# Attention and feed-forward in one kernel: the order of work drawn up again, with other planner costs and limits

## The chip, the cores and the metric

The kernel runs on one core of a Trainium2 chip. The metric is the device time of one execution in microseconds (us). The time before is the median of three runs. The profile is one execution of the same program.

## The reference

Two parts follow each other. First attention: 8 batches, 8 heads, 576 tokens, 64 values per head. The keys and values have 16 extra "beacon" rows in front, which every token sees; among the 576 tokens a token sees itself and those before it. Then a gated feed-forward step over all 4608 tokens: 512 values in, 1536 hidden, 512 out.

```python
k_all = np.concatenate([beacon_k, k], axis=2)          # 16 + 576 rows
scores = scale * np.matmul(q, k_all.transpose(0, 1, 3, 2))
scores = np.where(causal, -1000000000.0, scores)       # beacon columns stay open
scores = scores - scores.max(-1, keepdims=True)
a = np.exp(scores)
a /= a.sum(-1, keepdims=True) + 1e-09
attn = np.matmul(a, v_all)
x = attn.transpose(0, 2, 1, 3).reshape(4608, 512)
out = (np.maximum(x @ w_gate, 0.0) * (x @ w_val)) @ w_out
```

## The kernel before

**Tiling.** The heads of a batch are taken in four pairs, so that one product carries two heads. The queries of a pair lie in a tile `diag`: 64 queries of one head on partitions 0 to 63, 64 of the other on partitions 64 to 127, zeros elsewhere. The scores of 64 tokens of both heads are then one product of 128 rows. The rows of a batch are cut into the blocks A (with the beacon rows), B, C, D and E, 128 rows each or nearly so, and F, the last 16 tokens, for all four pairs at once.

**One step of attention** (`tile_step`, L616 on, and `group`, L713 on). PE makes scores in a PSUM bank (L663; L655 for E, L658 for F in column tiles of 32). DVE adds the mask and takes the minimum (L678, L675). ACT takes the exponential, with its sum (L689). DVE makes the reciprocal (L701). POOL multiplies by it (L708). The result is turned, in batch 0 by PE (L743) and later by a DMA transpose (L754). PE multiplies by the values (L764 in column tiles of 64, L793 for F), and DVE or ACT copies into `xT` (L440, L438).

**Loads.** In each batch SP's queue brings `k0` to `k3` and `q0` to `q3` (one per pair of heads), `v0` to `v4` (blocks of values), `F` (first rows: the first queries and beacon keys) and `L` (last rows). The order is written by hand in `ORDER0` for batch 0, `ORDER1` for batch 1 and `ORDER` for the others. Each load is cast to bf16 (L486, or L442 for values), by an engine of `CASTS` in batch 0 and by POOL later. Keys and queries are then turned by PE (L497) and copied out of the PSUM bank. A query has two copies, one for each half of the partitions (`evict_q`). The nine pieces of the weights are fetched from POOL's queue (L455), each not before a date: `W_FROM` and then every `W_STEP`.

**Feed-forward.** `hidden` makes, for each of 12 blocks, a product with the gate weights and one with the value weights (L831), ACT's relu (L835) and DVE's multiply (L839). `project` multiplies by the third weight (L851), the result is copied to `osb` and stored. The first three batches are cut at 240 columns of 512 (`CUTS`). So feed-forward's first product needs blocks A and B of all four pairs of batch 0.

**Order.** Nothing of the order is written by hand but the lists above. `Plan.order` is a list scheduler that runs while the kernel is built: each `Task` has engines, a planned cost, the tasks it depends on, and the tiles it holds. The scheduler always takes the task that can start first by the planned times; among equals, the one with the lower `prio`. The instructions are then issued in that order. The chip's engines take their own instructions in order, and wait by semaphores; the planned times are not carried to the chip. The functions `c_dve`, `c_exp`, `c_act`, `c_pool` and `c_pe` are planned costs for n columns.

All of PSUM's eight banks belong to one pool, `banks` (one of them is reserved for fillers in the beginning). `F_MOST`, `SC_MOST`, `V_MOST`, `FIRST_MOST` and `SC_FIRST` limit how many of them feed-forward, scores, products with values, and the first batch may hold at once. Where PE would stand idle early on, the scheduler puts in fillers, products that nobody reads (L910). `LAZY` and `LAZY1` keep a product with values waiting, once it is ready, so that several can follow each other: PE's column tiles change between 128 and 64 there. `RANK`, `AHEAD`, `STEPS`, `WHOLE`, `F_RANK`, `HOLD` and `PACE` are priorities and earliest dates of loads and steps.

```python
key = (at, late, t.prio)
...
late = -1 if part and t.part else 1 if not part and at < (could if SLOT_LAZY else t.ready) + t.lazy else 0
```

Of the kernel before, what the change touches and what calls it, by code (L numbers as in the profile page):

```python
# [20 lines left out]
RANK = (-1.46, -25.77, -19.88, -17.37)  # L21
AHEAD = (-24.27, 8.0, -0.29, 8.0)
W_ISSUE = 0.8
W_MOVE = 3.1
W_FROM = 14.62
W_STEP = 2.67
PACKET = 0.005
W_FIRST = 0.9
W_LEAD = 0.7
W_EACH = 3.3  # L30
W_DELAY = 0.5
W_LATE = 0.6
# [6 lines left out]
SWITCH = 0.1  # L39
LAGS = {"PE": 0.22, "ACT": 0.16, "DVE": 0.14, "POOL": 0.1, "DMA": 0.1}  # L40
LAZY = 22.34
LAZY1 = 32.19
SLOT_LAZY = 0
# [3 lines left out]
F_MOST = 5  # L47
# [3 lines left out]
V_MOST = 5  # L51
OUT = -1300.0
ZERO1 = 25.0
ORDER0 = "q0 q1 F k0 k1 k3 v1 q3 k2 q2 v2 v3 L v0 v4"
ORDER1 = "k0 F q0 k2 L k3 q2 v3 q3 k1 v0 v2 q1 v1 v4"
ORDER = "q0 k1 L k0 F q3 k3 q1 v1 k2 v0 v4 v3 q2 v2"
N_ST = 7
F_RANK = (6.53, 8.48, -1.67, 11.78)
CASTS = ('POOL', 'DVE')
N_OSB = 4  # L60
STEPS = {0: [(['AB'], (-4.55, -4.2, -4.25, -5.72)), (['C'], (-2.2, 4.89, 0.9, 1.36)), (['D', 'E'], (-0.26, 1.73, 10.1, -3.41))],
         1: [(['AB'], (4.7, -5.26, -1.44, -4.08)), (['C'], (8.45, 11.63, 1.33, -5.23)), (['D', 'E'], (3.48, 1.1, 9.61, 4.15))],
         2: [(['AB'], (6.63, 0.38, 0.63, -2.81)), (['C', 'D', 'E'], (6.95, 10.43, 5.74, -0.2))]}
WHOLE = (0.99, 5.23, 4.5, 5.2)
CUTS = {0: (240,), 1: (240,), 2: (240,), 3: ()}
LAST_PARTS = 2
FIRST_MOST = 4
PACE0 = 0.0
HOLD = {0: (0.0, 0.0, 0.0), 1: (0.0, 0.0, 35.39)}
PACE = 31.01  # L70
# [50 lines left out]
class Task:  # L121
    def __init__(self, engines, cost, run, deps, holds, prio, lag, part=False, lazy=0.0, move=0.0):
# [23 lines left out]
class Plan:  # L146
# [7 lines left out]
    def add(self, engines, cost, run, deps=(), holds=(), prio=0.0, lag=None, part=False, lazy=0.0, after=0.0, move=0.0):  # L154
        t = Task(engines if isinstance(engines, tuple) else (engines,), cost, run, deps, holds, prio, lag, part, lazy, move)
        t.ready = after
        for d in t.deps:
            d.users.append(t)
        self.tasks.append(t)
        return t  # L160

    def order(self):
# [13 lines left out]
        part = False  # L176
# [3 lines left out]
        def begin(t, e):  # L180
# [9 lines left out]
            return max(at, free[e]), at  # L190

        while True:
            best = None
            for e in queue:
                for t in queue[e]:
# [3 lines left out]
                    at, could = times  # L199
                    late = 0  # L200
                    if e == "PE":
                        late = -1 if part and t.part else 1 if not part and at < (could if SLOT_LAZY else t.ready) + t.lazy else 0
# [11 lines left out]
            if e == "PE" and FILL_FROM < at < self.filled:  # L214
# [3 lines left out]
                if n > 0 and tile is not None:  # L218
                    done.append(Filler(n, tile, self.fill))
            t.start, t.engine = at, e  # L220
# [22 lines left out]
            else:  # L243
                if isinstance(cost, dict):
                    cost = cost[e]
                if e == "PE":
                    cost = cost * (2.0 if at < WARM else 1.012) + SWITCH * (t.part != part)
# [20 lines left out]
def kernel(  # L268
# [93 lines left out]
    def c_exp(n):  # L362
        return 0.255 + 0.0009 * n
# [4 lines left out]
    def c_pool(n):  # L368
        return 0.245 + 0.00083 * n

    def c_pe(n):
        return 0.003 + n / 2400.0
# [95 lines left out]
    def new_batch(b, prio, work):  # L468
# [45 lines left out]
        def load_pair(kind, p, prio):  # L514
# [20 lines left out]
            def evict_q(hh):  # L535
# [3 lines left out]
                def run(x):  # L539
# [7 lines left out]
            t.rows[kind, p] = [add(("ACT", "DVE"), {"ACT": c_act(512) + (0.0 if kind == "k" else 0.12), "DVE": c_dve(512)},  # L547
                                   evict if kind == "k" else evict_q(i), (tu, zeros), (ps, dst), prio[1]) for i in range(halves)]

        def load_rest(kind, prio):  # L550
# [24 lines left out]
            def evict_q(x, hh):  # L575
# [8 lines left out]
            t.rows["q", kind] = [add(("ACT", "DVE"), {"ACT": 0.06 + c_act(n), "DVE": 0.06 + c_dve(n)}, lambda x, hh=hh: evict_q(x, hh),  # L584
                                     (tu, on_zeros.get(b)), (ps, t.diag), prio[1]) for hh in range(2)]
# [30 lines left out]
    def tile_step(t, p, name, ph, sc, prio, after, blocks):  # L616
# [48 lines left out]
        s = add("PE", pe, scores, deps, (sc[0], sc[1], ph, t.kT, t.diag), prio, None, part=name == "F", after=after)  # L665
# [37 lines left out]
        r = add("DVE", 0.15, inverse, sums, (), prio, 0.18)  # L703
# [240 lines left out]
```

## Time and profile before

| what | value |
|---|---|
| median of three runs | 410.61 us (410.17 to 411.67) |
| the profiled execution's own time | 409.49 us |
| its span, first to last instruction | 407.8 us |
| PE busy | 393.8 us (97%), 3276 products recorded |
| DVE, ACT, POOL busy | 320.7, 289.3, 232.6 us |
| first feed-forward product | 28.68 us from the span's start |
| last product | starts at about 402 us |
| TensorE's clock | 0.998 |

The times of the profile are counted from the span's start. PE counts as busy while products are in its pipeline, so a full PE is not a PE at its peak. Idle time of an engine is put down to what ended it. A line of the chain of waits gives start, duration and what ran; a line of the timeline gives start, duration, engine, line, operation, tiles and count, and, in brackets, the idle time before and what ended it.

### The profile page before, as it was taken

The numbers are of one execution on the slowest core, as the hardware profiler recorded it, in microseconds if no ns is written. First come the engines' busy times: TensorE is split into PE (matmuls) and PEld (weight loads), VectorE is DVE, ScalarE is ACT, GpSimd is POOL, SyncE is SP. The second block draws the span as 40 slices with busy tenths as digits, with TensorE's granted clock in tenths as the row PEclk, the third lists the DMA queues.
The fourth block names the chain that finished last, engine by engine and source line by source line (L and its number), as shares of the span: only waits on it lengthen the run. The fifth ranks groups of instructions, "written<-read, shape, count | busy, mean of one in ns | idle before, by whom it ended". The sixth has DMA issues, their size and how long they took to land.

```text
span 407.8 us, 10376 instructions
## 1 busy us (share of the span) xinstructions
PE 393.8 (97%) x3276; PEld 247.2 (61%) x3311; DVE 320.7 (79%) x1159; ACT 289.3 (71%) x959; POOL 232.6 (57%) x434
## 2 busy tenths in 40 slices
PE   7899999999999999999999999999999999999994
PEld 5567867587767877554558744654554544444483
DVE  6899999989989988899998998887988544244251
ACT  6899989789888968797888799898867432033040
POOL 5799786958686758576875956885727200000000
PEclk9999999999999999999999999999999999999999
DMA  7999999999899999899989999999195720200112
GB/s 230 161 206 223 212 210 197 196 233 216 172 205 231 189 196 225 193 239 210 211 193 214 235 186 193 247 201 214 41 162 125 173 67 0 75 29 0 53 54 51
DMA packets 172616, 68.03 MB, mean 167 GB/s; under 512 B 146832, under 2 KB 168080, under 8 KB 172560
## 3 DMA queue, kind: packets, MB, share of 16 engines
q1 hardware_dynamic: 167808, 62.64, 75.9%
q0 software_dynamic: 4752, 4.72, 7.2%
q8 instruction: 26, 0.43, 0.4%
q14 instruction: 30, 0.25, 0.2%
HBM read 38.27 MB, written 9.44 MB: 117 GB/s over the span
## 4 chain that ended last, share of the span: by engine, by line
PE 83%; POOL 5%; DVE 4%; DMA 4%; ACT 2%; issue 2%; SPq 0%; POOLq 0%; DVEq 0%; ACTq 0%
PE f L831 42%; PE f L851 21%; PE f L663 6%; PE f L764 6%; PE f L497 3%; DMA st<-in_v_dram 3%; POOL xT L708 2%; PE f L655 2%; DVE diag L440 1%; PE f L793 1%; POOL h L486 1%; DMA st<-in_q_dram 1%; DVE f L678 1%; PE f L658 1%; POOL pb L708 1%
## 5 line engine op out<-in xcount | busy, mean ns | idle before, releaser
L708 POOL TENSOR_SCALAR pb<-pb,small 128x576 bf16<-128x576 bf16 (+8 forms) x224 | 121.6, 557 | 59.1 <-DVE small L701 50.3
L689 ACT ACTIVATE pb<-f,small 128x64 bf16<-128x64 f32 (+6 forms) x256 | 131.1, 524 | 20.1 <-DVE small L678 16.1
L678 DVE CUSTOM_DVE_ANT_0 f<-f,mask 128x128 f32<-128x128 f32 (+7 forms) x256 | 112.0, 477 | 7.9 <-PE f L663 5.7
L835 ACT ACTIVATE g<-f 128x512 f32<-128x512 f32 (+3 forms) x156 | 71.8, 470 | 65.0 <-PE f L831 64.0
L831 PE MATMUL f<-xT,wv_r 128*128 128x512 bf16 (+3 forms) x616 | 111.8, 313 | 0.5
L831 PE MATMUL f<-xT,wg_r 128*128 128x512 bf16 (+3 forms) x619 | 109.5, 313 | 0.3
L839 DVE TENSOR_TENSOR hT<-g,f 128x512 bf16<-128x512 f32 (+3 forms) x156 | 80.2, 520 | 36.4 <-PE f L831 33.6
L851 PE MATMUL f<-wo_r,hT 128*128 128x512 bf16 (+1 forms) x423 | 102.0, 373 | 1.0
L831 PEld LDWEIGHTS <-wg_r 128*128 128x128 bf16 x624 | 60.0, 98 | 32.5 <-issue 0.2
L831 PEld LDWEIGHTS <-wv_r 128*128 128x128 bf16 x624 | 59.4, 98 | 32.9 <-issue 0.7
L851 PEld LDWEIGHTS <-hT 128*128 128x128 bf16 x444 | 41.5, 98 | 39.1
L689 ACT ACTIVATION_READ_ACCUMULATOR pb<-f,small 128x1 f32 x256 | 53.9, 210 | 0.0
L663 PE MATMUL f<-kT,diag 128*128 128x384 bf16 (+7 forms) x255 | 47.1, 286 | 3.0 <-DVE diag L440 1.6
L678 DVE DVE_READ_ACCUMULATOR2_ANT small<- 128x1 f32 x296 | 41.5, 140 | 0.2 <-issue 0.2
L486 POOL TENSOR_SCALAR h<-st 128x512 bf16<-128x512 f32 x62 | 37.7, 615 | 3.5 <-DMA st<-in_q_dram 1.3
L440 DVE COPY osb<-f 128x512 f32<-128x512 f32 (+1 forms) x26 | 17.6, 677 | 23.0 <-PE f L851 22.7
L708 POOL TENSOR_SCALAR xT<-xT,small 128x64 bf16<-128x64 bf16 (+4 forms) x64 | 27.0, 436 | 9.6 <-ACT xT L689 4.1
L663 PEld LDWEIGHTS <-diag 128*128 128x128 bf16 x256 | 20.4, 98 | 16.3 <-DVE diag L440 2.3
L438 ACT CAST diag<-f 64x512 bf16<-64x512 f32 (+2 forms) x52 | 23.0, 442 | 9.8 <-DVE diag L440 4.2
L497 PE MATMUL f<-ident,h 128*128 128x128 bf16 (+2 forms) x320 | 28.1, 217 | 1.2 <-POOL h L486 0.6
L440 DVE CAST diag<-f 64x512 bf16<-64x512 f32 (+2 forms) x44 | 26.3, 597 | 3.5 <-ACT diag L438 2.0
L689 ACT ACTIVATE xT<-f,small 128x64 bf16<-128x64 f32 (+5 forms) x64 | 27.8, 452 | 1.0 <-DVE small L678 1.0
(67 smaller groups left out, 377.2 us busy)
## 6 DMA issues: line engine op xcount, KB each, us to landing
st<-in_q_dram SPq DMA_DIRECT2D x32, 256.0 KB, 4.3
st<-in_k_dram SPq DMA_DIRECT2D x32, 256.0 KB, 4.5
out_dram<-osb SPq DMA_DIRECT2D x32, 256.0 KB, 2.5
st<-in_v_dram SPq DMA_DIRECT2D x24, 256.0 KB, 4.8
st<-in_v_dram SPq DMA_DIRECT2D x8, 224.0 KB, 4.9
wg_r<-in_moe_w_gate_dram POOLq DMA_DIRECT2D x3, 512.0 KB, 8.2
wv_r<-in_moe_w_val_dram POOLq DMA_DIRECT2D x3, 512.0 KB, 10.2
wo_r<-in_moe_w_out_dram POOLq DMA_DIRECT2D x3, 512.0 KB, 13.6
```

The lines of the kernel that those rows point to most:

```text
L440: nc.vector.tensor_copy(dst, src)
L486: (nc.gpsimd if x.engine == "POOL" else nc.vector).tensor_scalar(to, of, by, 1.0, ALU.mult, ALU.mult)
L497: nc.tensor.matmul(to, h16.tile[:rows, a * P:(a + 1) * P], ident[:rows, :rows], start=True, stop=True)
L663: nc.tensor.matmul(view(i), t.diag.tile[:, p, j * P:j * P + P], kT[:, p, :n], start=True, stop=True)
L678: nc.vector.tensor_tensor_reduce(out=view(i), in0=view(i), in1=msk, scale=1.0, scalar=small["t"][:, 0:1] if name in "EF" else 3.0e38, op0= ...
L689: nc.scalar.activation(ph.tile.rearrange("p a n -> p (a n)")[:, a:a + n], view(i), AF.Exp, bias=small["t"][:, low:low + 1], scale=-1.0, ac ...
L708: (nc.gpsimd if x.engine == "POOL" else nc.vector).tensor_scalar(one, one, small["t"][:, 8 + i:9 + i], 1.0, ALU.mult, ALU.mult)
L764: nc.tensor.matmul(ps.tile[64 * hh:64 * hh + 64, d0:d0 + w], t.v.tile[:rows, c, D * h:D * h + D], rhs(64 * hh), start=(c == 0), stop=(c == ...
L831: nc.tensor.matmul(to, w_r[:, ki, nf * P:(nf + 1) * P], x, start=(ki == 0), stop=(ki == KM - 1))
L835: r = add("ACT", c_act(w), lambda _, psg=psg, g=g: nc.scalar.activation(g.tile[:, :w], psg.tile[:, :w], AF.Relu), (a,), (psg, g), -1000 + ...
L839: hid.append(add("DVE", c_dve(w), lambda _, psv=psv, g=g, nf=nf: nc.vector.tensor_mul(hT[nf].tile[:, c0:c0 + w], g.tile[:, :w], psv.tile[: ...
L851: nc.tensor.matmul(ps.tile[:, :w], hT[nf].tile[:, t0:t0 + P], wo_r[:, nf, n0:n0 + w], start=(nf == 0), stop=(nf == NF - 1))
```

## The change

The planner's costs, lists, dates and limits get other numbers, and some of its rules change. The instructions of the kernel stay, but for their order, the choice among allowed engines, and the fillers.

- The two copies of a query out of one bank, and the three copies of a first or last row, get a dependency on each other in the plan.
- The planned costs of the exponential, POOL's multiply, PE's products, the reciprocal and the copies of turned blocks change, and PE's factor of 1.012 becomes `PE_RATE` of 0.998.
- `ORDER0` begins with `k1`; the other orders, the priorities, dates and paces get other values.
- Feed-forward may hold four banks (five before), products with values seven (five), the first batch's turns six (four). ACT may cast in batch 0.
- A product with values and an F score no longer belong to one kind: an F product with values has no waiting time and no kind of its own, F's scores are kind 3, and products with values kind 1. After a filler the kind is reset.

```diff
-RANK = (-1.46, -25.77, -19.88, -17.37)
-AHEAD = (-24.27, 8.0, -0.29, 8.0)
-W_ISSUE = 0.8
-W_MOVE = 3.1
-W_FROM = 14.62
-W_STEP = 2.67
-PACKET = 0.005
+RANK = (-7.1, -27.26, -24.83, -20.12)
+AHEAD = (-15.22, 1.47, 8.0, 7.48)
+W_ISSUE = 0.834
+W_MOVE = 3.3
+W_FROM = 15.63
+W_STEP = 2.53
+PACKET = 0.004
...
+PE_RATE = 0.998
-LAZY = 22.34
-LAZY1 = 32.19
-SLOT_LAZY = 0
+LAZY = 29.32
+LAZY1 = 11.61
...
-F_MOST = 5
+F_MOST = 4
-V_MOST = 5
+V_MOST = 7
-ORDER0 = "q0 q1 F k0 k1 k3 v1 q3 k2 q2 v2 v3 L v0 v4"
-ORDER1 = "k0 F q0 k2 L k3 q2 v3 q3 k1 v0 v2 q1 v1 v4"
-ORDER = "q0 k1 L k0 F q3 k3 q1 v1 k2 v0 v4 v3 q2 v2"
+ORDER0 = "k1 q0 q1 F k0 v2 v0 v1 q3 q2 k2 k3 v4 L v3"
+ORDER1 = "k0 q3 k2 q2 k3 F k1 q0 v4 v2 q1 v3 L v1 v0"
+ORDER = "k1 L F k0 q0 q3 k3 q1 k2 v0 v4 q2 v1 v3 v2"
-F_RANK = (6.53, 8.48, -1.67, 11.78)
-CASTS = ('POOL', 'DVE')
+F_RANK = (0.33, 8.02, 9.62, 8.82)
+CASTS = ('POOL', 'DVE', 'ACT')
-STEPS = {0: [(['AB'], (-4.55, -4.2, -4.25, -5.72)), (['C'], (-2.2, 4.89, 0.9, 1.36)), (['D', 'E'], (-0.26, 1.73, 10.1, -3.41))],
+STEPS = {0: [(['AB'], (-6.0, -1.43, -5.75, -2.97)), (['C'], (2.99, -2.13, 9.09, 9.58)), (['D', 'E'], (8.05, -5.08, 8.37, -1.22))],
...
-FIRST_MOST = 4
+FIRST_MOST = 6
-HOLD = {0: (0.0, 0.0, 0.0), 1: (0.0, 0.0, 35.39)}
-PACE = 31.01
+HOLD = {0: (0.0, 18.37, 0.0), 1: (41.75, 0.0, 0.0)}
+PACE = 32.26
...
-                    if e == "PE":
-                        late = -1 if part and t.part else 1 if not part and at < (could if SLOT_LAZY else t.ready) + t.lazy else 0
+                    if e == "PE" and t.part:
+                        late = -2 if part == t.part else -1 if part else 1 if at < t.ready + t.lazy else 0
...
-                    cost = cost * (2.0 if at < WARM else 1.012) + SWITCH * (t.part != part)
+                    cost = cost * (2.0 if at < WARM else PE_RATE) + SWITCH * (t.part != part)
...
     def c_exp(n):
-        return 0.255 + 0.0009 * n
+        return 0.23 + 0.00087 * n
     def c_pool(n):
-        return 0.245 + 0.00083 * n
+        return 0.24 + 0.00083 * n
     def c_pe(n):
-        return 0.003 + n / 2400.0
+        return 0.002 + n / 2400.0
...
-            t.rows[kind, p] = [add(("ACT", "DVE"), {...},
-                                   evict if kind == "k" else evict_q(i), (tu, zeros), (ps, dst), prio[1]) for i in range(halves)]
+            t.rows[kind, p] = []
+            for i in range(halves):
+                t.rows[kind, p].append(add(("ACT", "DVE"), {...},
+                                           evict if kind == "k" else evict_q(i), (tu, zeros, *t.rows[kind, p]), (ps, dst), prio[1]))
...
-        s = add("PE", pe, scores, deps, (sc[0], sc[1], ph, t.kT, t.diag), prio, None, part=name == "F", after=after)
+        s = add("PE", pe, scores, deps, (sc[0], sc[1], ph, t.kT, t.diag), prio, None, part=3 if name == "F" else 0, after=after)
...
-        r = add("DVE", 0.15, inverse, sums, (), prio, 0.18)
+        r = add("DVE", 0.08, inverse, sums, (), prio, 0.25)
...
-                     part=True, lazy=LAZY if t.b > 1 else LAZY1 * t.b)
+                     part=0 if what == "F" else 1, lazy=0.0 if what == "F" else LAZY if t.b > 1 else LAZY1 * t.b)
```

## The prediction

> **What bounds the kernel now.** I read the page first: the busy slices and the chain that ended last, by engine.
>
> ```profile
> PE   7899999999999999999999999999999999999994
> DVE  6899999989989988899998998887988544244251
> ACT  6899989789888968797888799898867432033040
> POOL 5799786958686758576875956885727200000000
> ...
> PE 83%; POOL 5%; DVE 4%; DMA 4%; ACT 2%; issue 2%; SPq 0%; POOLq 0%; DVEq 0%; ACTq 0%
> ```
>
> TensorE (PE) is the bound, and from slice 32 on it is alone: the attention engines fall off near 322 us. The table of windows says when PE fills up, and its line L910 (fillers) and the shapes say how much of a full PE is work.
>
> ```profile
> 10.00:20.00 10.00, 8.12 (x82) 6.12 (x81) 8.90 (x43) 7.98 (x33) 7.63 (x16) 1.00 1.02 163
> 20.00:30.00 10.00, 9.51 (x105) 6.48 (x105) 9.80 (x42) 10.00 (x38) 9.82 (x19) 1.00 1.15 204
> 30.00:40.00 10.00, 9.77 (x129) 7.45 (x123) 9.03 (x33) 9.36 (x29) 9.82 (x16) 1.00 1.20 224
> 50.00:60.00 10.00, 9.94 (x84) 7.39 (x82) 9.91 (x39) 8.55 (x35) 7.99 (x18) 1.00 1.23 219
> ```
>
> Columns (window, PE busy, PEld, DVE, ACT, POOL, clock, DMA, GB/s). In the chain, "323.67 8.20 PE f L831 x38" gives 0.216 us for a product of 512 columns, 0.42 ns per column. All columns without fillers (counted by the code, since some records are missing) cost 366 us at that pitch. So of the span of 407.8 some 42 us are not products. By 50 us only 25 us of products are done: 25 of the 42 are lost there. After the last product (402.3 us) come copy and store, 5.5 us, which the diff leaves alone. Between 50 and 403 us there remain some 11 us. So I need two sums: the start, and the small losses after it. The chain through the start, in order of time:
>
> ```profile
> 12.48 0.46 ACT diag L438
> 12.96 0.70 DVE diag L440
> ...
> 14.95 0.55 DVE diag L440
> 15.52 0.58 ACT diag L438
> 16.12 0.97 ACT xT L689 x4
> ...
> 17.70 0.68 POOL h L486
> 18.39 0.74 POOL xT L708 x2
> 19.13 0.59 POOL v L442
> 19.72 0.74 POOL wv_r L455
> ```
>
> Two query copies that read one bank after another, then exponentials, then GpSimd (POOL), which works without a gap from 17.4 to 46.9 us. The first feed-forward product starts at 28.68 us. The waits view names the pairs (total, times, longest):
>
> ```profile
> ACT diag L438 <- DVE diag L440: 4.2, 7, 1.5
> DVE diag L440 <- ACT diag L438: 2.0, 4, 0.8
> ```
>
> **The change part by part.** Nearly all of it alters the planner, so instructions and bytes stay and the order moves. "−" is a gain.
>
> *Copies of one bank follow each other.* The chip does that already: ACT 12.35–12.94, DVE from 12.96; DVE until 15.49, ACT idle 1.46 us until 15.52. The old plan thought both halves ran at once and parked an engine there. The new plan can put other work before the second half. On the chain the parked times are 0.40 and 1.46, so −1.9 at most; at worst the second half comes one exponential later (+0.7). I take −0.9, half of the bound, since all four pairs want ACT at that time. The halves lie in partitions 0–63 and 64–127. The Trainium skill (PSUM — Partial Sum Buffer, "PSUM bank collisions raise a hardware error") says that two engines may use different quadrants of a bank at once; by that the wait would be the program's own, the old plan's picture could be had, and this dependency would gain 0 (sum −1.9). The rows show the second copy waiting, and I go by them.
>
> *ACT may cast in batch 0.* POOL's chain holds two casts of batch 0, 0.68 and 0.59. Gone from there: −1.3. But ACT is busy 10.00 of 10 from 20 us, so a cast on it there costs its 0.55. Ends −1.3 to +0.55; I take −0.4.
>
> *Weights.* The first date goes from 14.62 to 15.63, the last (eight steps) from 35.98 to 35.87. First issues land at 21.75 and 25.26 us and are used at 28.68 and 30.25: 5 us of cover, cost 0; without it +1.0. Each issue holds POOL 0.79; the fifth, issued 27.52 (2.2 after its date of 25.30), moves to about 28, where it may fall behind the last norm the first products need: −0.8 to 0, I take −0.1.
>
> *Load order.* The first five loads are the same set (q0 q1 F k0 k1); only k1 leads, so the first pair still needs four of them: 0. Behind them three values now stand before pairs 2 and 3. In landings of before, the last load that the four pairs need came at 11.85 us (eleven landings at 0.75 to 1.3 us each); it will be the twelfth, near 13.9: +2.05 if that decides. The fourth pair's scores ran only at 18.59 us, some 4 us after load, cast, transpose and copy could be through. Hidden: 0. SP issues all fifteen by 13.7 us either way.
>
> *Dates.* Block C of batch 0 is held to 18.37. Before, the minimums of the first C ran at 11.97 and 13.89 us, 0.45 and 0.49 of DVE between those of A and B: −0.9 if they leave. But D and E of pair 1 now rank −5.08, ahead of A and B of pairs 1 and 3 (−1.43, −2.97), and may take the place: I take −0.2. A and B of batch 1, held to 41.75, were scored at about 45: 0.
>
> *Waits of PE after 50 us.* Only two are real: 0.58 idle at 60.58 (a POOL cast) and 0.56 at 185.36 (a query copy); with their surroundings 1.46. I take −0.7; a new order can as well make two of its own (+1.5).
>
> *Grouping P@V, F apart.* After 50 us PE changes 39 times between column tiles of 128, 64 and 32, each about 0.108 beyond its columns: 4.2. Longer patience for batches 2 to 7 (29.3 against 22.3) may save four bursts of two changes (−0.9); shorter for batch 1 (11.6 against 32.2) may add three (+0.65). I take −0.2.
>
> *Planned durations.* No instruction gets shorter. Rows against old and new figures: exponential of 64, 256, 512 columns starts the next after 0.29, 0.45, 0.66 (old 0.31, 0.49, 0.72; new 0.29, 0.45, 0.68); reciprocal 0.073–0.084 (0.15; 0.08); 512-column product 0.216 (0.219; 0.215). By 28 us some 45 exponentials were planned 0.035 too long: 1.6 us by which later steps were placed wrongly. I take −0.5, ends −1.6 to 0. PE's 1.3% over 350 us is 4.7 us in the plan, but on the chip shows only as the two waits above.
>
> *Feed-forward 4 banks, values 7, first steps 6.* With four, an eviction must end within three groups of the next products: 2.6 us at 512 columns, 1.24 at 240 (0.412 each). DVE's multiply takes 0.61 and 0.32. DVE waited for products here 33.6 us in all, so it is mostly early. I take +0.2; ends 0 and the rival's price below.
>
> *Sum:* −0.9 −0.4 −0.1 −0.2 −0.7 −0.2 −0.5 +0.2 = −2.8 us. A gain in the start carries fully, because PE is full from 50 us on and 80 us of feed-forward alone follow 322; the later weights keep their cover (the ninth block's products ran at 47.99, landed 38.38). The profiled execution took 409.49 us; 406.7 for its like. The median lies 1.1 higher, 410.61: **407.8 us**.
>
> **The rivals.**
>
> *Not carried (no change, 410 us).* POOL's chain from 17.4 to 46.9 us keeps its norms (0.29 to 0.73 each) and nine issues, and batch 1's loads land up to 42.8 us in a full DMA. If these pace the start, only mid-stream −0.7 is left: 409.9. For it: POOL 9.82 of 10. Against: its chain is fed late, by the two query pairs. That the program's waits already put the copies in order, so that the new dependency does nothing, leads here too.
>
> *Four banks hold PE (slower).* In the 240-, 256- and 272-column stages (144 groups), slack is 1.24 − 0.32 − 0.2 = 0.7 us: one DVE minimum of 0.60 (512 columns) ahead of the multiply fits, two do not. That is where it decides. If two stand ahead once in six groups, 24 stops of about 0.25 us make +6; with the other gains left, −3.0+6 = +3.0: 413.6. For it: DVE 9.9 of 10 at 50–60 us. Against: DVE idles 33.6 us for products. The Trainium skill (Perfetto Trace Analysis, "Matmul Optimizations") wants all eight PSUM banks used; this cap speaks against that, though the three to four others go to attention. No row here shows a cap of four.
>
> *Late pairs (slower).* Pairs 2 and 3 come 2.05 us later, their minimums and exponentials pile up behind 16 us where ACT is full, and the weights' 1.0 loses its cover: 410.6+3.0−0.7 = 412.9. Decides if the fourth pair's scores move beyond 20 us.
>
> **How the numbers follow.** Forecast 0.49, not carried 0.27, four banks 0.14, late pairs 0.10. Within 0.5% (about what a measurement tells apart here; 2.05 us) is 408.6 to 412.7. The forecast's own range is 405 to 409.3: the full bounds of start and switches (−1.9 −1.3 −0.9 −1.5) reach −5.6. About a tenth of it ends above 408.6, and as much of "not carried" below; so faster 0.47, same 0.29, slower 0.24. Of the slower cases the cheaper half belongs in the range: 404.8 to 413.6.
>
> **What would show it.** Right: the idle time of ACT and DVE for each other's diag copies falls from 6.2 us to under 3; the first L831 product starts before 28 us; products done by 50 us rise from 25 to 27; PE idle between 50 and 322 us stays under 3; the last product ends at about 400. Wrong: the first product at 28.5 or later; fewer products by 50 us; PE waiting in the 240-column stages for hT or g; more than 45 changes of column tile.

## The result, and the profile after

The changed kernel takes 413.18 us (median of five runs, 412.42 to 414.29), against 410.61 before: a ratio of 1.0058, interval 1.0035 to 1.0082. Forecast were 407.8. The profiled execution took 413.18 us with a span of 411.4, that of before 409.49 and 407.8.

The page of after, the busy slices and the chain by engine:

```profile
PE   7899999999999999999999989999999999999994
DVE  6899989898989889889789898997895844233251
ACT  5898999786979899797669787874884853033040
POOL 5799769657695688568748874982761620000000
...
PE 60%; DVE 3%; issue 2%; POOL 1%; ACT 1%; DMA 1%; SPq 0%; POOLq 0%; ACTq 0%; DVEq 0%
```

The chain of after can be followed back only to 125.18 us, so its shares add up to some 70% and are not to be set against the 83% of before. TensorE (PE) is still the bound (busy 396.4 of 411.4 us), and the last recorded product starts at 405.60 us instead of 401.98. The table of windows (window, PE busy, PEld, DVE, ACT, POOL, clock, DMA, GB/s):

```profile
10.00:20.00 10.00, 8.87 (x91) 6.99 (x91) 8.61 (x39) 8.13 (x28) 7.20 (x12) 1.00 0.84 168
20.00:30.00 10.00, 9.44 (x103) 6.56 (x100) 9.73 (x44) 10.00 (x39) 9.51 (x21) 1.00 1.18 223
30.00:40.00 10.00, 9.16 (x118) 7.04 (x116) 9.61 (x35) 8.40 (x30) 9.73 (x15) 1.00 1.20 231
50.00:60.00 10.00, 9.95 (x86) 7.39 (x85) 9.28 (x48) 9.05 (x38) 5.78 (x13) 1.00 0.69 153
```

PE is busier from 10 to 20 us (8.87 against 8.12), but less than half of what it holds there is work: 3.2 us of it are products that count, against 2.7; the fillers would take 4.1 us at single pitch in after and 4.2 in before. The measure that tells more is the one of the prediction, how far PE lies behind: the time gone, less the columns of all products but fillers that had started by then, at 0.42 ns each (products in column tiles of 64 or 32 run side by side and count by their share of the 128 columns). What it grows by is lost to waits, fillers, changes of column tile, or a slow clock. Some products are missing in the records (35 of 3221 before, 37 in after); each is counted where its weights were loaded. One product of 512 columns is 0.22 us, so differences below that mean nothing. In the profiles:

| at, us | before | after | a_t3 | a_t3l |
|---|---|---|---|---|
| 30 | 20.74 | 21.60 | 21.82 | 20.48 |
| 50 | 24.34 | 25.37 | 26.13 | 24.30 |
| 100 | 27.30 | 27.80 | 28.57 | 26.49 |
| 180 | 30.53 | 32.47 | 32.53 | 30.53 |
| 220 | 32.18 | 33.32 | 33.48 | 31.59 |
| 280 | 34.33 | 38.36 | 36.63 | 34.55 |
| 400 | 36.15 | 39.60 | 38.20 | 36.15 |

(a_t3 and a_t3l are experiments below.) By 400 us after is 3.45 us further behind. Two stretches make up more than that: the start, +1.03 us by 50, and 220 to 280 us, 5.04 instead of 2.15. The others nearly cancel: after wins 0.5 from 50 to 100 and 0.6 from 280 to 400 us, and loses 0.6 from 100 to 220 (1.4 up to 180, of which 0.8 come back). The experiments take the two stretches up after the suspects that the prediction had named. Times in microseconds are medians, and a ratio is to runs of before taken alongside, whose median moved between 410.22 and 410.97 from set to set; compare kernels by their ratios.

### The profile page after: what moved, and what is told of

Read it like the earlier page. It is cut to its first block, busy times and chain, and to the rows that moved or that the text cites. A ratio compares the mean times of both kernels' runs of the same rounds, so it can differ in the third digit from the quotient of the medians.

```text
span 411.4 us, 10350 instructions
## 1 busy us (share of the span) xinstructions
PE 396.4 (96%) x3278; PEld 249.2 (61%) x3315; DVE 320.4 (78%) x1163; ACT 287.0 (70%) x956; POOL 233.7 (57%) x433
## 4 chain that ended last, share of the span: by engine, by line
PE 60%; DVE 3%; issue 2%; POOL 1%; ACT 1%; DMA 1%; SPq 0%; POOLq 0%; ACTq 0%; DVEq 0%
PE f L838 32%; PE f L858 17%; PE f L670 4%; PE f L771 4%; PE f L498 2%; PE f L662 1%; DMA st<-in_beacon_v_dram 1%; ACT pb L696 1%; POOL pb L715 1%; DVE f L685 1%; PE f L800 1%; DVE diag L441 1%; DVE osb L441 0%; DVE small L703 0%; POOL h L487 0%
## 5 line engine op out<-in xcount | busy, mean ns | idle before, releaser
L685 DVE CUSTOM_DVE_ANT_0 f<-f,mask 128x448 f32<-128x448 f32 (+7 forms) x256 | 111.7, 474 | 6.5 <-PE f L670 5.0
L838 PE MATMUL f<-xT,wv_r 128*128 128x512 bf16 (+3 forms) x617 | 110.6, 313 | 0.8 <-ACT pb L696 0.4
L858 PE MATMUL f<-wo_r,hT 128*128 128x512 bf16 (+1 forms) x426 | 100.7, 373 | 0.9
L696 ACT ACTIVATION_READ_ACCUMULATOR pb<-f,small 128x1 f32 x256 | 55.0, 215 | 0.0
L670 PE MATMUL f<-kT,diag 128*128 128x128 bf16 (+4 forms) x255 | 46.0, 286 | 0.8 <-DVE hT L846 0.7
L441 DVE CAST diag<-f 64x512 bf16<-64x512 f32 (+2 forms) x52 | 28.5, 553 | 5.0 <-PE f L498 2.7
L498 PE MATMUL f<-ident,h 128*128 128x128 bf16 (+2 forms) x320 | 29.3, 220 | 3.2 <-POOL h L487 1.5
L498 PEld LDWEIGHTS <-h 128*128 128x128 bf16 (+2 forms) x320 | 21.5, 99 | 15.1 <-POOL h L487 4.4
L682 DVE TENSOR_REDUCE small<-f 128x1 f32<-128x512 f32 x40 | 27.3, 682 | 3.0 <-PE f L662 2.2
L696 ACT ACTIVATE xT<-f,small 128x64 bf16<-128x64 f32 (+3 forms) x64 | 27.6, 446 | 2.4 <-DVE small L685 1.7
```

Source lines behind the costliest of these rows:

```text
L441: nc.vector.tensor_copy(dst, src)
L498: nc.tensor.matmul(to, h16.tile[:rows, a * P:(a + 1) * P], ident[:rows, :rows], start=True, stop=True)
L670: nc.tensor.matmul(view(i), t.diag.tile[:, p, j * P:j * P + P], kT[:, p, :n], start=True, stop=True)
L682: nc.vector.tensor_reduce(out=to, in_=view(i), axis=AX.X, op=ALU.min)
L685: nc.vector.tensor_tensor_reduce(out=view(i), in0=view(i), in1=msk, scale=1.0, scalar=small["t"][:, 0:1] if name in "EF" else 3.0e38, op0= ...
L696: nc.scalar.activation(ph.tile.rearrange("p a n -> p (a n)")[:, a:a + n], view(i), AF.Exp, bias=small["t"][:, low:low + 1], scale=-1.0, ac ...
```

## Experiments: what it was not

**The cap of four banks.** `a_f5` is after with one line changed, `b_f4` is before with the other.

```diff
-F_MOST = 4
+F_MOST = 5
```

> The kernel after, with F_MOST back at 5 (feed-forward may hold five banks again); all else as after, 413.2 us. Theory 'four banks': the cap makes PE wait for banks, so with five the time falls to 410.5 or less and the waits of PE between 50 and 322 us fall under 3 us. Theory 'no slack' (the measured costs let PE's products stand right behind the casts and copies they need, and each small delay on the chip stops PE): the cap is not the cause, the time stays within 412 to 414 and PE's waits name POOL casts (h) and query copies (diag) as in the kernel after. Theory 'start' (the new loads of batch 0 cost 1.2 us by 50 us, the rest is chance): the start is as in after, 413 by 1 either way.

> The kernel before (410.6 us) with F_MOST 4 alone. 'Four banks': slower, 412.5 to 414, with multiplies (hT) and relus (g) ending PE's waits in the 240- and 272-column stages. 'No slack' and 'start': no change, 410 to 411.5, since a group's bank is back within 1.2 us and three groups of 240 columns last 1.24.

Measured: a_f5 413.14, ratio to before 1.0074 (1.0055 to 1.0094); b_f4 410.22, 1.0003 (0.999 to 1.0016). No price of the cap shows in either order. But a_f5 is another order, and loses in another place: 4.0 us from 150 to 180 us, where after loses 1.6 (PE waits 1.02 us at 178.28 for a copy into `xT`), and only 2.2 from 220 to 280, where after loses 5.0.

**The dependency between copies.** `a_nodeps` is after with the copies of one bank independent of each other in the plan again.

```diff
-            t.rows[kind, p] = []
-            for i in range(halves):
-                t.rows[kind, p].append(add(("ACT", "DVE"), {...},
-                                           evict if kind == "k" else evict_q(i), (tu, zeros, *t.rows[kind, p]), (ps, dst), prio[1]))
+            t.rows[kind, p] = [add(("ACT", "DVE"), {...},
+                                   evict if kind == "k" else evict_q(i), (tu, zeros), (ps, dst), prio[1]) for i in range(halves)]
```

> The kernel after without the dependency between the copies of one bank; the planner again takes them for parallel. If the dependency gains what I put on it (0.9 in the start and idle time of ACT and DVE for each other's diag copies), the time rises from 413.2 to 414 or more and those waits rise from some 2 us to 5 or more. If the chip's order of the copies is what counts and not the plan's picture of it, 413 by 0.7 either way. 'No slack': a plan that thinks the copies parallel is tighter still, so 414 to 415.

Measured: 418.26, 1.0189 (1.0164 to 1.0214). The waits view (engine line, what it waited for: total, times, longest) of after, and then of a_nodeps:

```profile
DVE diag L441 <- ACT diag L439: 0.5, 1, 0.5
```

```profile
ACT diag L439 <- DVE diag L441: 7.0, 9, 1.6
...
DVE diag L441 <- ACT diag L439: 2.2, 6, 0.8
```

Before it was 6.2 us, after it is 0.5, and 9.2 without the dependency. So that part of the change does to these waits what was forecast. With the lists of after the kernel is some 5 us slower without it, though the edit also draws the whole order anew, so the waits alone are not shown to cost that. It isn't what made the kernel slower.

**The planned durations.** `b_newcost` is before with all the new planned costs and its own lists, `b_rate` is before with PE's factor alone.

```diff
-                    cost = cost * (2.0 if at < WARM else 1.012) + SWITCH * (t.part != part)
+                    cost = cost * (2.0 if at < WARM else 0.998) + SWITCH * (t.part != part)
```

> The kernel before with the new planned costs alone (exponential, POOL multiply, reciprocal, turned copies, PE's product and factor), lists and limits as before. 'No slack': slower than 410.6 by 2 to 4 us, 412.5 to 414.5, and PE's waits between 50 and 322 us rise from 2.8 idle to 4 or more. If better costs give a better order, as I forecast: 408 to 410. 'Lists fitted to their costs' (priorities and dates were chosen for the old costs, and any redrawn order is worse by chance): also slower, but then the loss lies in the start and in other places than waits for casts.

> The kernel before with PE's factor 0.998 in place of 1.012 alone; priorities and dates as before. The plan gets 1.4% shorter on PE and nothing on the chip does. 'No slack': waits of PE after 50 us rise by 1 to 3 us over the kernel before, time 411.5 to 413.5. 'Lists fitted to their costs': a redrawn order, anywhere from 411 to 418, with most of the loss wherever the order happens to be worse, start included. If a truer PE cost gives a better order: under 410.

Measured: b_newcost 422.05, 1.0292 (1.0269 to 1.0315); b_rate 413.48, 1.0067 (1.0052 to 1.0081). b_rate keeps the start of before (24.63 us behind at 50) and loses later, above all between 220 and 280 us: 33.05 to 38.41 behind, 5.4 us where before loses 2.15. With the old lists, PE's new factor alone makes the kernel slower by as much as the whole change does, and all new costs together by five times as much. Lists and costs go together here: lists drawn up for one set of costs lost under another, twice.

## Experiments: 220 to 280 us

The timeline of after (start, duration, engine, line, operation, tiles, count; in brackets the idle time before and what ended it), PE and then POOL:

```profile
238.10 1.33 PE L498 MATMUL f<-ident,h 128*128 128x128 bf16 x12
239.26 1.03 PE L838 MATMUL f<-xT,wg_r 128*128 128x512 bf16 x4
...
241.07 0.38 PE L498 MATMUL f<-ident,h 128*128 128x128 bf16 x4
241.68 0.38 PE L498 MATMUL f<-ident,h 128*128 128x128 bf16 x4 [0.22 <-ACT diag L439]
242.51 1.02 PE L838 MATMUL f<-xT,wv_r 128*128 128x512 bf16 x4 [0.45 <-ACT pb L696]
```

```profile
237.00 2.96 POOL L487 TENSOR_SCALAR h<-st 128x512 bf16<-128x512 f32 x5
```

Five casts of a batch follow each other on POOL, 0.6 us each, and their turns (L498) follow each other on PE. Twelve turned blocks of 128 columns take 1.33 us there; a group of four takes 0.38. Each turn holds a PSUM bank until its copies are through. At 242.51 a feed-forward product waits 0.45 us, and what ends the wait is an exponential that has read its bank. Before has the turns apart, each between products of the third weight:

```profile
232.72 0.39 PE L497 MATMUL f<-ident,h 128*128 128x128 bf16 x4
232.94 1.03 PE L851 MATMUL f<-wo_r,hT 128*128 128x512 bf16 x4
233.81 0.61 PE L497 MATMUL f<-ident,h 128*128 128x128 bf16 x8
```

`e_turns` moves every turn of batches 1 to 7 back in PE's queue, until it stands at least 0.6 us (planned) behind its cast:

```diff
+    for t in [t for t in made if t.engine == "PE" and t.start > 50.0 and "turned" in t.run.__qualname__]:
+        ...                       # behind the last PE task with u.start < t.ready + 0.6
+        made.insert(to, made.pop(i))
```

> The kernel after with one thing moved: after 50 us, turns of keys and queries (L498) go later in PE's queue where they stood less than 0.6 us behind their cast in the plan; every other engine keeps its order. 'No slack': PE's waits for casts (130, 115, 240, 275 us in the kernel after, some 2.4 us with what is hidden in weight loads) go, the products done between 50 and 400 us gain 1.5 to 2.5 us, and the time falls from 413.2 to 411 to 411.7. If those waits only move (the copies come later and hold ACT, DVE and the scores behind them): 413 by 0.7. 'Start': the loss of 1.2 us by 50 us stays in either case.

Measured: 415.07, 1.0112 (1.0094 to 1.013). No wait of PE for a POOL cast over 0.2 us is left after 50 us, and others came: 0.76 us at 123.93 for a query copy, 0.44 at 245.98 that ends, as at 242.51 above, with an exponential. Here the wait was moved and not cured.

`a_lazy` puts `LAZY` back to 22.34, which redraws the order from 220 us on. `a_t3` gives the turns of later batches a limit of three banks:

```diff
+    t_ps = Share(banks, 3)
...
-            ps = Hold(first_ps if b == 0 else v_ps, 1 + users)
+            ps = Hold(first_ps if b == 0 else t_ps, 1 + users)
```

> The kernel after with LAZY put back from 29.32 to 22.34: the order of instructions is the same until about 220 us, and differs behind it. Theory (PSUM banks): between 236 and 243 us of the profile after, a burst of feed-forward turns and five POOL casts in a row holds PSUM banks, the feed-forward products find none, and TensorE falls behind by about 1.5 to 2 us between 220 and 260 us. With the old LAZY the turns are spread, so this loss goes and the time is 411.3 to 411.8. Rival (the attention's engines set the middle, whatever the turns do): the time stays at 413.2 within 0.5, and the 2 us are lost at another place behind 260 us. Rival (only a start carries): as the second.

> The kernel after with the turns of batches 1 to 3 held to at most three PSUM banks at a time by a limit of their own; the order is that of after until about 233 us. Theory (PSUM banks): a part of the loss between 236 and 243 us goes, 412.3 to 413.0, and the products behind 240 us start at least 0.5 us earlier against the same amount of work. Rival (the order behind 233 us is redrawn and any redraw is as good): within 0.5 of 413.2 on either side, with no gain between 236 and 243 us.

Measured: a_lazy 412.17, 1.0044 (1.0025 to 1.0062); a_t3 411.30, 1.0034 (1.0015 to 1.0054), more than expected. (The interval of a_t3 overlaps that of after, but ten of its twelve runs lie below all five of after.) a_t3's order is that of after until 233 us. PE in a_t3:

```profile
237.43 1.03 PE L859 MATMUL f<-wo_r,hT 128*128 128x512 bf16 x4
238.29 0.39 PE L499 MATMUL f<-ident,h 128*128 128x128 bf16 x4
238.78 1.02 PE L839 MATMUL f<-xT,wg_r 128*128 128x512 bf16 x4
...
242.61 1.89 PE L839 MATMUL f<-xT,wg_r 128*128 128x512 bf16 x8 [0.37 <-ACT pb L697]
```

The burst of twelve has become four and eight, with feed-forward in between. Between 220 and 280 us a_t3 falls 3.15 us further behind, after 5.04. Only a part of these 1.9 us is won at the burst: from 233 to 245 us after falls 2.4 us behind, a_t3 1.8 (before nothing). From 268 to 280 us it is 1.9 against 0.8. There after has a wait for a query copy inside its products with values, and twelve turned blocks that again take longer than in a_t3 (after, then a_t3):

```profile
273.62 1.60 PE L771 MATMUL f<-pTb,v 128*64 128x128 bf16 x32 [0.28 <-DVE diag L441]
275.15 1.16 PE L498 MATMUL f<-ident,h 128*128 128x128 bf16 x12
```

```profile
274.01 0.84 PE L499 MATMUL f<-ident,h 128*128 128x128 bf16 x12
```

So the limit is worth some 1.9 us in this stretch, but that held banks are the cause is not shown: it also draws the order behind 233 us anew, the wait at 242.61 stays, and a_lazy, another order without the limit, loses 3.4 us there, nearly as little as a_t3. What the profile of after shows is the place: where turns follow each other at the pace of their casts PE falls behind, and 0.67 us of idle time there (0.22 and 0.45) end with a copy and an exponential.

## Experiments: the start

`e_cast` moves one POOL cast of batch 0, that of the last key (16.53 us in after), two norms earlier. `a_lazyc` and `a_t3c` add the same to a_lazy and a_t3.

> The kernel after with one POOL instruction moved: the cast of the last pair's load in batch 0 (16.53 us) goes two norms earlier in POOL's queue. 'Late pairs' (the loads of pairs 2 and 3 stand behind three values, land up to 2.6 us later, and their casts fall behind norms in POOL's queue): the first feed-forward product comes 0.3 to 0.9 us earlier than 30.7 and the time falls by as much, to 412.3 to 412.9. If the start is paced by the sum of POOL's work and not by that pair: 413.2 by 0.4, first product at 30.7 still.

> The edit of a_lazy together with that of e_cast (the last pair's POOL cast in batch 0 stands two norms earlier in POOL's queue). If both causes are right and add up (1.2 us of the start, 1.5 to 2 us at 236 to 243 us): 410 to 411, within 0.1% of the kernel before. If a gain in the start does not carry: as a_lazy. If neither matters: 413.2.

> The edit of a_t3 (turns of later batches in at most three PSUM banks) together with that of e_cast (the last pair's POOL cast in batch 0 two norms earlier). Theory (two causes that add up: 1.2 us in the start, 1.9 us of held banks): against a_t3's 411.3 another 0.7 to 1.2 us less, 410.1 to 410.6, no different from the kernel before. Rival (what is won before 50 us is lost again between 100 and 200 us, as in e_cast and a_lazyc): 411.3 to 412.3, with products done by 50 us about 1 us further than in a_t3 and by 180 us no further.

Measured: e_cast 414.58, 1.0099 (1.008 to 1.0118); a_lazyc 412.82, 1.0071 (1.0045 to 1.0097); a_t3c 412.57, 1.0052 (1.0033 to 1.0072). None is faster than its like without the move. e_cast's profile looked like a success at first, 24.56 us behind at 50 instead of 25.37. That reading fell. a_t3l below has no edit ahead of 112 us and shows 24.30 there, while a_t3, with the same start, shows 26.13: the new start differs by up to 2 us from execution to execution. Ten profiles with the new order of loads and fillers show 24.30 to 26.46, 25.5 on average; before, b_f4 and b_rate show 24.24 to 24.63. So the new start costs about 1.1 us on average. And e_cast, whose order on PE is that of after, is level with after again by 180 us (32.47 both).

**What waits at 131 us.** Part of what an execution wins in the start it can lose here. PE, POOL and SP in a_t3c:

```profile
130.73 0.57 PE L839 MATMUL f<-xT,wv_r 128*128 128x240 bf16 x4
132.54 0.40 PE L499 MATMUL f<-ident,h 128*128 128x128 bf16 x4 [1.24 <-POOL h L488]
```

```profile
131.87 0.62 POOL L488 TENSOR_SCALAR h<-st 128x512 bf16<-128x512 f32 x1 [1.33 <-DMA st<-in_k_dram]
```

```profile
126.21 0.42 SPq L522 DMA_DIRECT2D st<-in_k_dram  x1
```

PE waits 1.24 us for a cast, the cast for a key, and the key was issued by SP at 126.21 behind transposes and two stores that had waited for other engines. Nothing held the load itself, as a_t3l shows below by issuing it at 117.93. In after the same wait is 0.44 us. `a_t3l` and `a_t3cl` move this load and the two beside it, in SP's queue alone, ahead of two transposes of xT, one of pTf and two stores:

```diff
 pTb<-pb   (transpose)
+st<-in_q, st<-in_k, st<-in_v
 xT<-xT x2, pTf<-pf   (transposes)
 out<-osb  (store)
-st<-in_q
 out<-osb  (store)
-st<-in_k, st<-in_v
```

> The kernel a_t3 with three loads (a query, a key, a block of values) moved ahead in SP's queue, from about 125 to 127 us to about 119 us, ahead of two transposes of xT, one of pTf and two stores; all other engines keep their order. Theory (the key load behind SP's transposes paces TensorE at 131 us in most executions): the load lands before 126 us, no wait of TensorE for a POOL cast between 125 and 135 us, and 0.3 to 0.8 us less than a_t3: 410.5 to 411.0. Rival (what is gained ahead of 130 us is lost at the next wait anyway; or the transposes, 2 us later now, delay the products with values): 411.3 or slower, up to 412.5.

> The same move of three loads in a_t3c (a_t3 with the last pair's POOL cast in batch 0 two norms earlier; 412.57, with a wait of 1.24 us at 132.5 us). Theory: this queue is what eats the start's gain: 410.0 to 410.8, and products done by 180 us at least 1.2 us further than in a_t3c. Rival (the cast's move itself costs elsewhere, whatever the queue): 411.8 to 412.6, with the wait of 1.24 us gone and the time lost at another place.

Measured: a_t3l 411.01, 1.0003 (0.9982 to 1.0023); a_t3cl 411.64, 1.0017 (0.9992 to 1.0042). In a_t3l:

```profile
117.93 0.42 SPq L522 DMA_DIRECT2D st<-in_k_dram  x1
...
119.42 3.11 SPq L762 DMA_TRANSPOSE xT<-xT  x2
```

The key lands at 121.9 us instead of 131.7 and 130.4 (a_t3c, after), and no wait of PE for a POOL cast is left between 120 and 140 us in either. Both kernels gain 0.3% against their like; the intervals of each pair overlap, so this gain is likely rather than shown. With it, a_t3l is level with the kernel before.

**Why the start varies.** Ahead of the third turn of batch 0 (a query's, whose load is third in the new order) the old order has seven fillers, the new one has one. Before, and then a_t3:

```profile
5.79 1.50 PE L910 MATMUL f<-mask,ident 128*128 128x256 bf16 x7
7.22 0.29 PE L497 MATMUL f<-ident,h 64*128 64x64 bf16 x4
```

```profile
5.44 0.27 PE L918 MATMUL f<-mask,ident 128*128 128x256 bf16 x1
7.78 0.40 PE L499 MATMUL f<-ident,h 128*128 128x128 bf16 x4 [2.07 <-POOL h L488]
...
9.54 1.04 PE L918 MATMUL f<-mask,ident 128*128 128x256 bf16 x4
10.36 0.63 PE L499 MATMUL f<-ident,h 128*128 128x128 bf16 x4
10.79 0.85 PE L918 MATMUL f<-mask,ident 128*128 128x256 bf16 x3
11.43 0.95 PE L671 MATMUL f<-kT,diag 128*128 128x448 bf16 x5
```

Soon after 2.07 us of idle time, fillers and turns at 9.5 to 11.4 us run at twice their pitch (0.213 us for 256 columns), and the granted clock of these windows says so:

```profile
8.00:9.00 1.00, 1.00 (x11) 0.69 (x7) 0.78 (x2) 0.00 (x0) 0.95 (x2) 0.72 1.18 185
9.50:11.40 1.90, 1.90 (x13) 1.47 (x12) 0.81 (x3) 0.58 (x2) 0.64 (x2) 0.50 1.18 227
```

Fourteen fillers stand between that turn and the first scores. In five of ten profiles with the new start they ran slowly and the first score product came at 10.90 to 11.80 us, in the other five at 9.09 to 9.62. In all ten the first products ran at twice their pitch. In the fast five that ended at 4.6 to 5.5 us, and the idle time ahead of the third turn was 0.81 to 1.56 us. In three of the slow (a_lazyc, a_t3, a_t3cl) it ended by 5.4 us too, but the idle time was 1.86 to 2.07 us, and the doubled pitch came back at 8.3 to 9.0 us. In two, after and e_turns, it lasted through to 10.5 and 13.7 us, with idle times of 0.52 and 1.48. So in after the slow fillers can't be put down to the idle time, ahead of which the doubled pitch had not ended. The Trainium skill ("TensorE: Matmul & The Clock Gate", "What's actually happening") says that the clock is set by free-running windows of about 3.4 us, and halves after an idle one. That would let one order meet either case, though the idle time here, 0.5 to 2.1 us, is shorter than such a window, and no run shows the windows. `a_t3l_p` puts six more fillers ahead of the third turn, `a_t3l_m` takes the fourteen away.

> a_t3l with six more fillers (256 columns each) ahead of the third turn of batch 0, where TensorE waits 0.5 to 2.1 us for a cast. Theory (that idle stretch brings the doubled pitch back, and the pitch holds the first scores): single pitch from about 7.5 us, first score product at 9.1 to 9.7, and the executions lie closer together; 410.0 to 410.7, against 411.0 for a_t3l, whose executions went from 409.4 to 413.0. Rival (the last key's landing paces the start, whatever the pitch): 411.0, same spread. Rival (the fillers are in the way): up to 411.6.

> a_t3l without the fourteen fillers between the third turn of batch 0 and the first score product. Theory: the doubled pitch has nothing left to stretch there, so the first score product comes at 9.1 to 9.7 us in any execution; 410.0 to 410.7. Rival (fewer fillers leave TensorE idle, so that the doubled pitch lasts into the scores): first score product early, but the scores and turns behind it at twice the pitch, 411 to 412. Rival (last key's landing): 411.0, same spread.

Measured: 411.55, 1.0013 (0.9995 to 1.0032), and 411.08, 1.0004 (0.9987 to 1.0021); a_t3l's 411.01 is not beaten. The first score product came early in both (9.64 and 9.03), as the theory said, though half of the profiles without these edits have it early too. In a_t3l_m the doubled pitch came back behind the first scores, as its rival said: the nine fillers there take 2.13 us (1.15 in a_t3l), at a granted clock of 0.50.

```profile
10.78 2.13 PE L918 MATMUL f<-mask,ident 128*128 128x256 bf16 x9
```

The first feed-forward product still came at 30.91 and 30.50. POOL in a_t3l_p suggests why:

```profile
14.50 1.24 POOL L716 TENSOR_SCALAR xT<-xT,small 128x64 bf16<-128x64 bf16 x3
15.98 0.62 POOL L488 TENSOR_SCALAR h<-st 128x512 bf16<-128x512 f32 x1 [0.24 <-DMA st<-in_k_dram]
```

That is the last key, k3, twelfth in the new load order, and POOL waits for it with norms and the weights' issue in its queue. Over all twelve profiles with the new start the first feed-forward product starts at the later of two times, first score + 19.9 us and k3's landing + 15.0 us (both constants are fitted to these profiles):

| profile | first score | k3 lands | later sum | first feed-forward |
|---|---|---|---|---|
| after | 10.96 | 14.46 | 30.86 | 30.69 |
| a_f5 | 9.52 | 16.02 | 31.02 | 30.80 |
| e_turns | 11.80 | 15.54 | 31.70 | 31.81 |
| a_t3 | 11.43 | 15.93 | 31.33 | 31.29 |
| a_t3l | 9.09 | 14.82 | 29.82 | 29.42 |
| a_t3l_p | 9.64 | 15.80 | 30.80 | 30.91 |
| a_t3l_m | 9.03 | 15.34 | 30.34 | 30.50 |

(a_t3l lies 0.4 us ahead of the sum; the five that are not shown lie within 0.2 us of it.) Before, the first feed-forward product follows the first score by 19.3 us, at 28.68, and its last pair's load lands at 11.85.

`a_t3l_k` and `a_t3l_pk` load k3 one place earlier, ahead of the third block of values, whose cast goes behind k3's.

> a_t3l with the third block of values (v1 in ORDER0) loaded behind the last key instead of ahead of the last two queries, and its POOL cast behind that key's cast. Theory (the last key's landing paces the start): it lands about 1 us earlier, 13.8 to 15.2 us, and the first feed-forward product starts by the later of first score + 19.9 and landing + 15.0, within 0.5; time 410.2 to 410.8 against 411.0. Rival (POOL: the cast that now lies between norms and the first weights' issue costs its 0.62 us): first product later than that by 0.5 or more, 411.0 to 411.6.

> The same with the six more fillers of a_t3l_p, so that the first score product comes early too. Theory: first score product by 9.7, first feed-forward product 29.2 to 30.0, time 409.9 to 410.5, as the kernel before or less. Rival (POOL's cast): 30.4 or later, 411.0 to 411.6.

Measured: 415.21, 1.0108 (1.0084 to 1.0131), and 414.27, 1.0097 (1.007 to 1.0124). These two don't decide it. The cast came to stand behind the next load into the same staging tile, so these kernels cast other rows of values in place of that block, and POOL waited for them:

```profile
18.94 0.62 POOL L444 TENSOR_SCALAR v<-st 128x512 bf16<-128x512 f32 x1 [3.42 <-DMA st<-in_v_dram]
```

k3 did land at 13.73, but 3.4 us of POOL hid what that is worth. They show one thing: a_t3l_k is 3.5 us further behind than a_t3l at 50 us and 4.1 at 400. This loss in the start is not made good later.

**Another list.** `s_b4` has the code of after, planned costs nearer to the rows, and lists drawn up for these costs.

```diff
-        return 0.002 + n / 2400.0
+        return 0.0027 + n / 2400.0
-PE_RATE = 0.998
+PE_RATE = 1.0
-SWITCH = 0.1
+SWITCH = 0.108
...                                # a turn not before 0.4 us behind its cast; RANK, ORDER0, STEPS and the other lists anew
```

> The code of after with planned costs nearer to the rows (product 0.0027 + n/2400 us with a factor of 1.0, a change of column tiles 0.108, a turn not before 0.4 us behind its POOL cast) and lists drawn up for these costs. Theory (a list is good only for the costs it was drawn up with, and the nearer these are to the rows the more of the plan arrives): 407 to 410, faster than both kernels; no wait of TensorE for a POOL cast between 50 and 325 us over 0.3 us. Rival (what is lost is waits that no cost in the plan describes, so any new order is as good as another): 411 to 415.

Measured: 410.42, 1.0008 (0.9994 to 1.0022), level with before, where its theory had expected it faster. Its start is among the worst (first feed-forward product at 31.75 us, 26.06 behind at 50) and its middle nearly as good as that of before (10.3 us lost from 50 to 280, before 10.0, after 13.0), with no wait of PE for a POOL cast over 0.3 us between 50 and 325. No kernel here is shown to beat the one before.

## Why the prediction was wrong, step by step

The sum forecast −2.8 us; measured were +2.6. Both the start and the stretch behind it went the other way, the second by more.

*A gain in the start, and that it carries.* Forecast 27 us of products by 50, from 25; there were 24.6 (before 25.7). Carrying was mostly right, in both directions: a_t3l, 1.8 us better than a_t3 at 50, is 2.0 better at 400, and a_t3l_k's loss stays; but the 0.8 us by which e_cast led after at 50 were gone by 180. There was no gain to carry: the first feed-forward product came at 30.69, not before 28, and the last product at 405.60, not at about 400. So the rival *not carried* (409.9) is no better than the forecast: it wasn't carrying that failed.

*Load order, 0.* This is the first step that failed: the start lost 1.03 us (some 1.1 on average of ten profiles) where the terms of the start promised a gain. It put the fourth key's landing near 13.9 us and hid it behind the fourth pair's scores at 18.59. It landed at 14.46 to 16.33, depending on the execution, and the fourth pair's scores ran at 19.86 in after; the third pair's, at 12.53 before, ran at 18.20. The cover was a product's start time, and everything between landing and that product (a POOL queue with norms in it, turn, two copies) was taken for free. The timeline shows POOL waiting for the key, up to 1.19 us in a_t3c. That the landing paces the start is an inference from twelve profiles; the experiment that was to decide it cast other rows, so it stays open.

*The first scores* were no step of the sum. The order of the first five loads also moved an idle stretch of PE and its fillers. In half of the profiles with it the fillers ran at twice their pitch and the first scores came up to 2 us later; why in one execution and not in another stays open. In after's it is the later of the two sums above, so by that rule it paces that start:

```profile
6.71 0.60 PE L498 MATMUL f<-ident,h 128*128 128x128 bf16 x4 [0.52 <-POOL h L487]
...
8.74 0.39 PE L498 MATMUL f<-ident,h 64*128 64x64 bf16 x4
...
10.96 1.22 PE L670 MATMUL f<-kT,diag 128*128 128x448 bf16 x9
```

*Copies, −0.9.* Right in kind (6.2 us of waits to 0.5), but what became free was taken by pair 1's D: its exponentials ran at 12.21 and 14.47 us, ahead of the other pairs' A and B. Ten exponentials instead of fourteen had started by 20 us. The step *dates* had seen that these might take the place, and put −0.2 on it. The Trainium skill's rule on quadrants ("PSUM — Partial Sum Buffer", "PSUM bank collisions raise a hardware error") would have made the dependency worth nothing; with the lists of after, the kernel without it has 8.7 us more of these waits and is 5 us slower.

*Weights, −0.1.* Their cover stayed, as forecast: the first two pieces landed at 23.20 and 25.92 us and were used from 30.69 on.

*ACT may cast, −0.4.* ACT took no cast of a key, query, F or L in batch 0: DVE took three, POOL seven. Worth 0.

*Waits of PE after 50 us, −0.7.* The second step that failed, and the larger: it counted two idle gaps of before and took a new order to have fewer, with a bound of +1.5 on the other side. The gaps over 0.19 us between 50 and 325 us add up to 1.65 us (1.14 before), and from 220 to 280 us after falls 2.9 us further behind than before, most of it not as idle time but as turns that run at the pace of their casts. The term looked at idle time alone and so had no place for this loss. A limit on the turns' banks, with the order that it brings, took back 1.9 us of it, and the move of three loads in SP's queue likely 0.3% of the whole; how much of the rest is held banks and how much is the new order stays open.

*Grouping.* 41 changes of column tile after 50 us, 39 before: 4.7 us beyond their columns for 4.2, so +0.5 instead of −0.2 (0.25 of it is the wait at 273.62).

*Planned durations, −0.5.* The sign was wrong for the lists of before (b_rate +0.7%, b_newcost +2.9%).

*Four banks, +0.2, and its rival at 413.6.* Nothing in either order; the rule to use all eight banks ("Perfetto Trace Analysis", "Matmul Optimizations" in the Trainium skill) is neither borne out nor refuted by the cap.

*Late pairs, 412.9, 0.10.* The nearest rival in time and in its first half. The fourth pair's scores ran at 19.86 us in after, just short of its sign of 20, and at 18.63 in a_t3l. Its price of 3.0 us in the start was too high for after (1.03), and the rest came from 220 to 280 us, so that its time comes so near is in part luck.

## What to carry to other kernels

A list that was drawn up against a planner's costs can lose when these costs change, even towards the truth: judge a new order as a whole, by what follows in bursts and by what stands behind a waiting instruction in each queue, the loading queue included, not by summing the edits. An experiment that changes a limit draws a new order too, so look at where it wins before its gain is put down to the limit. Before a moved load is called hidden, follow it through the cast's engine and its queue, and compare its landing over several executions. And before a gain within one profile is believed, look at a second profile of the same stretch.

## What the runs showed of the hardware

- Between executions of one order of loads the twelfth landed at 14.5 to 16.3 us. The first products ran at twice their pitch: until 4.6 to 5.5 us in five of ten profiles with the new start, in three more again from 8.3 or 9.0 to about 11 us, and in two through to 10.5 and 13.7 us. In three profiles with the old start it ended at about 5.3 to 7 us.
- In a_t3's windows the granted clock reads 0.50 while the pitch is doubled; in after's it reads 1.00 from 2 to 14 us, with the same doubled pitch at 9 to 10.5 us. The pitch of the fillers is the safer sign.
- After 50 us a change of column tile on PE (128, 64, 32) took 0.09 to 0.125 us beyond the columns, 0.11 in the middle (39 changes before).
